# Blockwise causal attention and a swish layer on one core: Q of batches 2 to 7 loaded with even and odd tokens in two planes

## The chip, the cores and the metric

One Trainium2 chip, one core. The metric is device time in microseconds, the median over runs of the whole kernel. Before the change it is 328.6 us (three runs, 328.39 to 328.95).

## What is computed

Attention over 8 batches of 8 heads, 576 tokens and a head width of 64, causal in blocks of 64 tokens, and behind it a two-layer block on the 4608 rows of 512 numbers that the heads give together:

```
scores = (q @ k.T) / 8                      # a token of block i sees the tokens of blocks 0 to i
attn   = softmax(scores)
x      = (attn @ v), heads side by side     # 4608 x 512
h      = x @ w_in                           # 512 -> 2048
g      = h * sigmoid(beta * h)
out    = g @ w_out                          # 2048 -> 512, float32
```

## The kernel before

The kernel is a list of operations that a planner (`Plan.schedule`, line 85) puts in order when the program is built. Each operation has an engine, a planned duration, dependencies and tiles. For DMAs there is a planned transfer time (`xfer`), and the planner models two rings, one for the hardware queue that SyncE (SP) feeds and one for GpSimd's. It hands every engine a fixed sequence; at run time nothing is chosen again, an engine waits on semaphores in that sequence. A change of a planned duration can therefore move any operation of any engine.

The attention works in units: `u = 4 * b + c` is the pair of heads `2c`, `2c + 1` of batch `b`. Batches 0 and 1 load Q and K in one way (line 724) and turn them with TensorE (line 742); the change leaves them alone. For batches 2 to 7 (`QB = 2`), two units, so four heads, go together and are called a quad here. There are 12 quads, and each goes through these steps:

- **Load** (line 765, on SP's queue): the 2304 rows of four heads' Q, 64 floats each, go to a tile `S4` of 128 partitions with 18 rows each, row `128 i + p` in partition `p`. So each piece that a DMA moves is one row of 256 B. K is loaded in the same way. Planned transfer `QKX = 2700` ns for each.
- **Cast** (line 776, GpSimd): four copies of 128x640, for each of two pairs of heads one for Q and one for K, from float32 to bf16, into a tile `QKn`.
- **Transpose** (line 783, a DMA on SP's queue, once all four casts are done): 20 blocks of 128x128 from `QKn` into `QKT`, after which the head dimension lies in the partitions, two heads in the two halves. Planned 3250 ns.
- **Scores** (line 837, TensorE; repeated with the weights kept, line 457): three visits for each quad. The two heads of a pair use the upper and the lower half of the array and write to two neighbouring PSUM banks. A visit has 4 or 12 instructions at line 837.
- **Exponential** (line 857, ScalarE): 128x1024 from the two banks to a tile `E`, three for each pair, and a small one of 128x128 (line 872). VectorE then zeroes the corners of the causal mask (lines 865 and 867).
- **Values** (line 1051, TensorE), the reciprocal of the sum (line 1063) and the product with it (line 1070, VectorE) into `xq`.
- **Transpose of the result** into `xT`: for batch 2 by TensorE and VectorE (lines 1099 and 1109), for batches 3 to 7 by a DMA on SP's queue (line 1087).

The second part runs over 9 chunks of 512 rows: `xT` times `w_in` (line 1297), tanh on ScalarE (line 1307), the gate on VectorE (line 1311), and the product with `w_out`: plain for the first chunk (line 1333), by seven products of quarter blocks with sums on VectorE (lines 1178 and 1214) for the others. The priorities (`pr`, line 452, for the attention; `1000 + 100 r + j` for chunk `r`) let the planner interleave the attention of a batch with the second part of chunks about one and a half batches behind.

SP's queue carries in one sequence the loads of Q, K and V, the transposes of Q and K, and those of `xq`. The output goes out on ScalarE's queue, the weights come in on GpSimd's. Two identity matrices are made by GpSimd at the start (lines 472 to 479); `identF` has 128 columns in float32, and its only use is a 16x16 transpose (line 512).

Of the kernel before, what the change touches and what calls it, by code (L numbers as in the profile page):

```python
# [6 lines left out]
f32 = mybir.dt.float32  # L7
# [352 lines left out]
def bass_blockwise_causal_attn__then__act_swish_beta_kernel(  # L360
# [10 lines left out]
    with es:  # L371
# [97 lines left out]
        def mk(fn):  # L469
# [4 lines left out]
            out=identF[:], in_=identF[:], compare_op=ALU.not_equal, fill=1.0, base=0,  # L474
            pattern=[[-1, 128]], channel_multiplier=1)), deps=[c1], prio=-9)
        c3 = P.op("POOL", 260, mk(lambda g: g.memset(identB[:], 0.0)), prio=-10)
# [177 lines left out]
        early6, rows = [], []  # L654
        QKI, QKX = 550, 2700
        for u in range(NU):
# [102 lines left out]
            elif p == 0:  # L759

                for w, (nm, src) in enumerate((("Q", q), ("K", k))):
                    ts = P.tile("S4")

                    def fl(g, e, ts=ts, src=src, b=b, c=c):
                        return [g.dma_start(STh[ts.slot], src[b, 2 * c:2 * c + 4].rearrange("h t d -> (h t) d").rearrange(
                            "(i p) d -> p i d", p=128))]

                    o = P.op("SP", QKI, fl, deps=[o for t in early6 for o in t.users] if b == QB else [],
                             tiles=[ts], xfer=QKX, prio=u, dma=["d_S4", 0, 1])
                    for i in range(2):  # L770
                        ld[nm, u + i] = o
                    for a in range(2):
                        def fn(g, e, ts=ts, tn=tn, a=a, w=w):
                            x = STh[ts.slot][:, 9 * a:9 * a + 5, :]
                            x = bass.AP(x.tensor, x.offset, [x.ap[0], [64, 5], [256, 2], [1, 64]])
                            return g.tensor_copy(  # L776
                                QKn[tn.slot][:].rearrange("p a w n -> p (a w n)")[:, 640 * (2 * a + w):][:, 0:640]
                                .rearrange("p (t h d) -> p t h d", t=5, h=2), x)

                        casts.append(P.op(CAST, 740, fn, deps=[o], tiles=[ts, tn], prio=u))  # L780

                def ft(g, e, tn=tn, td=tt_):
                    return [g.dma_start_transpose(QKT[td.slot][:].rearrange("c a w (t n) -> c (a w t) n", n=128),
                                                  QKn[tn.slot][:].rearrange("p a w n -> p (a w n)")[:, 0:2560])]
# [6 lines left out]
            if b not in JOIN or p == 0:  # L791
# [6 lines left out]
                for grp in visits:  # L798
# [5 lines left out]
                    def fq(g, e, pst=pst, grp=grp, tqk=tqk, b=b):  # L804
# [8 lines left out]
                        while todo[0] or todo[1]:  # L813
# [4 lines left out]
                            m = 128 if t < 4 or b >= QB else 64  # L818
                            if g0 < 3:
# [8 lines left out]
                            x = QKT[tqk.slot][r, uu % 2, 0, q0 + y:q1 + y]  # L828
                            if b and g0 == 1 and (uu, 0) in grp and t == 0:
                                z = again(g, o, keep[h], x)  # L830
                                continue
                            if g0 == 3 and h and last is not None:
# [18 lines left out]
            for g0 in range(4 if b else 3):  # L851
                o, ps = qk[g0]
                if g0 < 3:
                    n = 512 if b or g0 < 2 else 256

                    def fe(g, e, ps=ps, g0=g0, te=te, n=n):
                        return g.activation(E3[es_(te)][:, g0, :, 0:n], PS[:, ps.slot:ps.slot + 2, 0:n], ACT.Exp,  # L857
                                            scale=0.125)
# [10 lines left out]
                else:  # L869
                    def fe(g, e, ps=ps, te=te, p=p):  # L870
                        n = 128 if te.apart else 64
                        return g.activation(E4[es_(te)][:, 0:n], PS[:, ps.slot, n * p:n * p + n], ACT.Exp, scale=0.125)
                    n = 128 if te.apart else 64
# [553 lines left out]
```

## Time and profile before

| | |
|---|---|
| median of three runs | 328.6 us |
| the profiled execution's own time | 329.3 us |
| its span, first to last instruction | 327.5 us |
| TensorE busy in the span | 316.4 us, 97% |
| ScalarE, VectorE, GpSimd busy | 211.8, 219.9, 84.5 us |
| granted TensorE clock | 0.999 of full speed |
| bytes moved | 53.58 MB, 164 GB/s over the span |

The busy time of an engine is the union of its instructions' durations; a matmul's duration overlaps the next one's, so a TensorE that is busy all the time still has small gaps between streams. The profiled execution took 329.3 us, 1.8 us more than its span and 0.7 us more than the median of the runs. DMA-issuing instructions stand under the queue of the engine that issues them (SPq, ACTq, POOLq); their time is the sequencer's, and it is long when the queue is full.

### The profile page before, as it was taken

How to read it: one execution, taken by the hardware profiler on the slowest of the kernel's cores; microseconds unless marked ns; L12 is line 12 of the kernel's file. 1: busy time of each engine (PE TensorE's matmuls, PEld its weight loads, DVE VectorE, ACT ScalarE, POOL GpSimd, SP SyncE). 2: the span in 40 equal slices, each digit the busy share in tenths (PEclk: the TensorE clock that was granted, in tenths of full speed). 3: DMA queues.
4: the chain of work that ended last, by engine and by line, in shares of the span. 5: the costliest groups of instructions: out<-in, count | busy, mean ns of one | idle time of the engine just before them, and what ended most of it. 6: DMA issues, size and time to landing. Idle time of an engine off the chain costs nothing.

```text
span 327.5 us, 7435 instructions
## 1 busy us (share of the span) xinstructions
PE 316.4 (97%) x3101; PEld 200.3 (61%) x3012; DVE 219.9 (67%) x455; ACT 211.8 (65%) x312; POOL 84.5 (26%) x137
## 2 busy tenths in 40 slices
PE   7698999999999999999999999999999999999996
PEld 2454446445786457854776467666666766666695
DVE  5657857578763789368843996659576866666742
ACT  2769891388557886499657866885978454544521
POOL 4768090073073046103520541150000000000000
PEclk9999999999999999999999999999999999999999
DMA  7999999999999999997999999999030310111023
GB/s 224 225 302 233 215 211 199 169 292 189 226 252 221 222 193 218 186 240 152 196 190 241 231 197 195 199 169 152 0 74 2 104 34 32 62 36 35 6 92 128
DMA packets 156706, 53.58 MB, mean 164 GB/s; under 512 B 139120, under 2 KB 156160, under 8 KB 156672
## 3 DMA queue, kind: packets, MB, share of 16 engines
q1 hardware_dynamic: 144112, 40.46, 65.8%
q10 hardware_dynamic: 8336, 8.46, 8.2%
q0 software_dynamic: 4224, 4.19, 7.8%
q8 instruction: 24, 0.39, 0.5%
q14 instruction: 10, 0.08, 0.1%
HBM read 36.71 MB, written 9.44 MB: 141 GB/s over the span
## 4 chain that ended last, share of the span: by engine, by line
PE 83%; DMA 5%; DVE 4%; ACT 4%; issue 2%; SPq 1%; POOL 1%; POOLq 0%
PE PS L1297 34%; PE PS L1214 29%; PE PS L1051 8%; PE PS L837 6%; PE PS L1333 4%; DMA w_in<-in_moe_w_in_dram 3%; ACT E L857 2%; DMA ST<-in_q_dram 2%; DVE gT L1311 1%; ACT th L1307 1%; DVE QKT L752 1%; SPq L724 1%; DMA xT<-xq 1%; PE PS L1099 1%; PE PS L912 0%
## 5 line engine op out<-in xcount | busy, mean ns | idle before, releaser
L1297 PE MATMUL PS<-xT,w_in 128*128 128x512 bf16 x576 | 137.7, 379 | 3.1 <-DMA w_in<-in_moe_w_in_dram 1.2
L1307 ACT ACTIVATE th<-PS,beta 128x512 f32<-128x512 f32 x144 | 97.0, 701 | 54.9 <-PE PS L1297 53.9
L1311 DVE SCALAR_TENSOR_TENSOR gT<-th,PS 128x512 f16<-128x512 f32 x144 | 95.2, 681 | 35.8 <-ACT th L1307 35.4
L857 ACT ACTIVATE E<-PS 128x1024 bf16<-128x1024 f32 (+1 forms) x90 | 87.5, 1014 | 22.4 <-PE PS L837 21.5
L1297 PEld LDWEIGHTS PS<-xT,w_in 128*128 128x128 bf16 x576 | 53.1, 98 | 58.5 <-issue 2.2
L1214 PE MATMUL PS<-w_out,gT 128*128 128x256 f16 x512 | 63.0, 273 | 0.1
L1214 PEld LDWEIGHTS PS<-w_out,gT 128*128 128x128 f16 x512 | 49.0, 98 | 12.1 <-issue 0.8
L776 POOL CAST QKn<-ST 128x640 bf16<-128x640 f32 x48 | 37.0, 771 | 24.9 <-DMA ST<-in_k_dram 13.9
L624 POOL CAST Vn<-Vs 128x640 bf16<-128x640 f32 x24 | 19.6, 815 | 91.7 <-DMA Vs<-in_v_dram 90.6
L1236 ACT ACTIVATE ost<-PS 128x512 f32<-128x512 f32 x32 | 19.3, 604 | 28.5 <-PE PS L1214 28.5
L1214 PE MATMUL PS<-OV 128*128 128x256 f16 (+1 forms) x264 | 31.8, 270 | 0.0
L1051 PEld LDWEIGHTS PS<-Vn,E 128*128 128x128 bf16 x810 | 27.5, 97 | 3.9 <-issue 0.4
L837 PE MATMUL PS<-QKT 64*128 64x448 bf16 (+7 forms) x292 | 28.6, 295 | 0.5 <-ACT E L857 0.5
L1051 PE MATMUL PS<-Vn,E 128*128 128x65 bf16 x810 | 28.4, 193 | 0.0
L1214 PEld LDWEIGHTS PS<-OV 128*128 128x128 f16 x264 | 24.5, 98 | 6.1 <-issue 0.6
L1178 DVE TENSOR_TENSOR OV<-gT 128x1024 f16<-128x1024 f16 x32 | 23.9, 753 | 0.6
L837 PEld LDWEIGHTS PS<-QKT 64*128 64x128 bf16 (+1 forms) x292 | 13.3, 94 | 17.7 <-issue 3.6
L1070 DVE TENSOR_TENSOR xq<-PS,inv 128x640 bf16<-128x640 f32 x28 | 23.0, 820 | 0.5
L1239 DVE SCALAR_TENSOR_TENSOR ost<-PS,ost 128x512 f32<-128x512 f32 x22 | 15.2, 689 | 9.5 <-PE PS L1214 6.9
L865 DVE MEMSET E<- 64x64 uint32 x57 | 6.3, 112 | 17.9 <-ACT E L857 16.0
L1214 PE MATMUL PS<-OV,gT 128*128 128x256 f16 (+1 forms) x136 | 16.0, 266 | 0.0
L1333 PE MATMUL PS<-w_out,gT 128*128 128x512 f16 x64 | 15.3, 379 | 0.0
(106 smaller groups left out, 189.9 us busy)
## 6 DMA issues: line engine op xcount, KB each, us to landing
out_dram<-ost ACTq DMA_DIRECT2D x32, 256.0 KB, 3.9
ST<-in_q_dram SPq DMA_DIRECT2D x12, 576.0 KB, 6.2
ST<-in_k_dram SPq DMA_DIRECT2D x12, 576.0 KB, 7.2
Vs<-in_v_dram SPq DMA_DIRECT2D x24, 256.0 KB, 4.6
ST<-in_q_dram SPq DMA_DIRECT2D x8, 256.0 KB, 5.9
ST<-in_k_dram SPq DMA_DIRECT2D x8, 256.0 KB, 6.1
w_in<-in_moe_w_in_dram POOLq DMA_DIRECT2D x4, 512.0 KB, 8.4
w_out<-in_moe_w_out_dram POOLq DMA_DIRECT2D x4, 512.0 KB, 8.9
```

What stands on the lines that cost most here:

```text
L624: return g.tensor_copy(Vn[t.slot][:, 0:n, g0:g1, 0:64], Vs[ts.slot][:, 0:n, g0:g1, :])
L776: return g.tensor_copy(QKn[tn.slot][:].rearrange("p a w n -> p (a w n)")[:, 640 * (2 * a + w):][:, 0:640] .rearrange("p (t h d) -> p t h d ...
L837: z = g.matmul(o, QKT[tqk.slot][r, uu % 2, 1, k0:k0 + m], x)
L857: return g.activation(E3[es_(te)][:, g0, :, 0:n], PS[:, ps.slot:ps.slot + 2, 0:n], ACT.Exp, scale=0.125)
L1051: z = g.matmul(o, eblk(te, t, i, h), Vn[Tv.slot][:, t, 2 * c + h, 0:65], start=(t == 0), stop=(t == i))
L1070: return g.tensor_tensor(xq[xq_(tx)][:].rearrange("p i (h d) -> p h i d", h=2), both(pv, 0, 64), x, ALU.mult)
L1178: return P.op("DVE", dve_t(SZ * HC / 2), mk(lambda g: g.tensor_tensor(fo(), fx(), fy(), op)), deps=deps, tiles=tiles, prio=prio)
L1214: x = g.matmul(PS[:, pw.slot, HM * w + c0:HM * w + c1], fa()[:, j, 128 * w:128 * w + 128], fb()[:, j, c0:c1], start=first and (pair or w = ...
L1297: z = g.matmul(PS[:, ph.slot, :], w_in[:, c, 128 * j:128 * j + 128], xT[:, c, row % RX:row % RX + RC], start=(c == 0), stop=(c == 3))
L1307: return g.activation(th[tt.slot][:], PS[:, ph.slot, :], ACT.Tanh, scale=beta[:, j:j + 1])
L1311: return g.scalar_tensor_tensor(out=gT[tg.slot][:, j, :], in0=th[tt.slot][:], scalar=1.0, in1=PS[:, ph.slot, :], op0=ALU.add, op1=ALU.mult)
L1333: z = g.matmul(PS[:, po.slot, 0:d1 - d0], gT[tg.slot][:, j, 128 * w:128 * w + 128], w_out[:, j, d0:d1], start=(j == 0), stop=(j == NJ - 1))
```

## The change

For batches 2 to 7, Q is loaded with two neighbouring tokens in each partition, so that a piece is 512 B. The even and the odd tokens of a head then lie in two planes after the cast: a head's 576 tokens start at partition 0, 32, 64 or 96 of their first block of 256 tokens, so three blocks of two planes are kept for each pair of heads, 768 columns where there were 640. The casts of Q become four of 128x384 for each quad instead of two of 128x640. `QKn` and `QKT` grow from 2560 to 2816 columns, so the transpose has 22 blocks. The score matmul reads its moving operand from the two planes and writes the even tokens' scores to the first half of a bank and the odd ones' to the second; the exponential reads the two halves alternating and writes the tokens in their order. K stays as it is. The planned transfer of Q becomes 2000, the planned transpose 3550, a planned Q cast 470. In SBUF, `identF` shrinks to 16 columns and batch 0's tile `QKt` moves into `OV`.

```diff
-        QKn = [sb(f"QKn{i}", [128, 2, 2, 640], bf16) for i in range(NQ)]
-        QKt = [sb("QKt", [128, 2, 256], bf16), OV[:, 512:768].bitcast(bf16).rearrange("p (w n) -> p w n", w=2)]
+        QKnf = [sb(f"QKn{i}", [128, 2816], bf16) for i in range(NQ)]
+        QKn = [x[:, 0:2560].rearrange("p (a w n) -> p a w n", a=2, w=2) for x in QKnf]
+        QKt = [OV[:, z:z + 256].bitcast(bf16).rearrange("p (w n) -> p w n", w=2) for z in (2048, 512)]
-        QKT = [sb(f"QKT{i}", [128, 2, 2, 640], bf16) for i in range(3)]
+        QKTf = [sb(f"QKT{i}", [128, 2816], bf16) for i in range(3)]
+        QKT = [x[:, 0:2560].rearrange("p (a w n) -> p a w n", a=2, w=2) for x in QKTf]
...
-        identF = sb("identF", [128, 128], f32)
+        identF = sb("identF", [128, 16], f32)
...
-        QKI, QKX = 550, 2700
+        QKI, QKX, QKX2 = 550, 2700, 2000
...
+                    def fl(g, e, ts=ts, src=src, b=b, c=c, w=w):
+                        x = src[b, 2 * c:2 * c + 4].rearrange("h t d -> (h t) d")
+                        if w == 0:
+                            return [g.dma_start(STh[ts.slot].rearrange("p (i j) d -> p i (j d)", j=2),
+                                                x.rearrange("(i p j) d -> p i (j d)", p=128, j=2))]
+                        return [g.dma_start(STh[ts.slot], x.rearrange("(i p) d -> p i d", p=128))]
...
-                             tiles=[ts], xfer=QKX, prio=u, dma=["d_S4", 0, 1])
+                             tiles=[ts], xfer=QKX if w else QKX2, prio=u, dma=["d_S4", 0, 1])
...
+                        for j in range(2 - w):
+                            def fn(g, e, ts=ts, tn=tn, a=a, w=w, j=j):
+                                x = STh[ts.slot][:, 9 * a if w else 8 * a + j, :]
+                                x = bass.AP(x.tensor, x.offset, [x.ap[0], [64, 5] if w else [128, 3], [256, 2], [1, 64]])
+                                y = QKnf[tn.slot][:, 1408 * a + 768:1408 * a + 1408] if w else \
+                                    QKnf[tn.slot][:, 1408 * a + 384 * j:1408 * a + 384 * j + 384]
+                                return g.tensor_copy(y.rearrange("p (t h d) -> p t h d", h=2, d=64), x)
+
+                            casts.append(P.op(CAST, 740 if w else 470, fn, deps=[o], tiles=[ts, tn], prio=u))
...
-                turned = [P.op("SP", 3250, ft, deps=casts, tiles=[tt_, tn], xfer=3200, prio=-1, dma=["d_T", 0, 1])]
+                turned = [P.op("SP", 3550, ft, deps=casts, tiles=[tt_, tn], xfer=3500, prio=-1, dma=["d_T", 0, 1])]
...
+                            n2 = (q1 - q0) // 2
+                            if b >= QB and g0 < 3:
+                                o = PS[:, ps.slot + h, :].rearrange("p (j n) -> p j n", j=2)[:, :, off // 2:off // 2 + n2]
...
-                                o = PS[:, ps.slot, k:k + 64]
+                                o = PS[:, ps.slot, k:k + 64].rearrange("p (j n) -> p j n", j=2)
...
+                            if b >= QB:
+                                s0 = 64 * (uu % 2) + 32 * h + q0 // 2
+                                x = QKTf[tqk.slot][r, 1408 * (uu % 2):1408 * (uu % 2) + 1408]
+                                x, kt = x[:, 0:768].rearrange("c (j n) -> c j n", j=2)[:, :, s0:s0 + n2], x[:, 768 + k0:768 + k0 + m]
...
-                            z = g.matmul(o, QKT[tqk.slot][r, uu % 2, 1, k0:k0 + m], x)
+                            z = g.matmul(o, kt, x)
...
+                        if b >= QB:
+                            return g.activation(E3[es_(te)][:, g0].rearrange("p h (n j) -> p h n j", j=2),
+                                                PS[:, ps.slot:ps.slot + 2].rearrange("p h (j n) -> p h n j", j=2), ACT.Exp, scale=0.125)
...
+                        if te.apart:
+                            x, y = x.rearrange("p (h n j) -> p h n j", h=2, j=2), y.rearrange("p (h j n) -> p h n j", h=2, j=2)
+                        return g.activation(x, y, ACT.Exp, scale=0.125)
```

## Rows read from the trace of the kernel before

**Rows 1.** The page: busy time of each engine, and the chain's shares by engine.

```profile
PE 316.4 (97%) x3101; PEld 200.3 (61%) x3012; DVE 219.9 (67%) x455; ACT 211.8 (65%) x312; POOL 84.5 (26%) x137
...
PE 83%; DMA 5%; DVE 4%; ACT 4%; issue 2%; SPq 1%; POOL 1%; POOLq 0%
```

**Rows 2.** Busy time in stretches: length, PE, PEld, DVE, ACT, POOL, clock, DMA share, GB/s.

```profile
35.00:222.00 187.00, 184.88 (x1884) 115.33 (x1837) 128.17 (x274) 132.81 (x196) 62.31 (x80) 1.00 1.12 209
45.00:251.00 206.00, 204.25 (x2082) 129.15 (x2033) 143.28 (x300) 145.36 (x214) 58.08 (x75) 1.00 1.01 188
251.00:311.00 60.00, 60.00 (x451) 39.90 (x450) 41.45 (x67) 31.78 (x50) 0.00 (x0) 1.00 0.14 42
```

**Rows 3.** Waits of TensorE's matmuls from 45 us on: total us, times, longest.

```profile
PE PS L1297 <- DVE xT L1109: 0.6, 1, 0.6
PE PS L1297 <- DMA xT<-xq: 0.6, 1, 0.6
PE PS L1297 <- DVE gT L1311: 0.2, 1, 0.2
PE PS L837 <- ACT E L857: 0.2, 1, 0.2
```

**Rows 4.** The two longest of these in TensorE's timeline: start, us, idle before.

```profile
104.32 1.04 PE L1297 MATMUL PS<-xT,w_in 128*128 128x512 bf16 x4 [0.62 <-DVE xT L1109]
...
170.92 1.90 PE L1297 MATMUL PS<-xT,w_in 128*128 128x512 bf16 x8 [0.61 <-DMA xT<-xq]
```

**Rows 5.** DMA view of 2 to 10 us, and of 88.5 to 98 us.

```profile
DMA packets 3353, 2.38 MB, mean 297 GB/s; under 512 B 1310, under 2 KB 3353, under 8 KB 3353
...
DMA packets 7562, 2.35 MB, mean 248 GB/s; under 512 B 7177, under 2 KB 7433, under 8 KB 7561
```

**Rows 6.** SP's queue: start, us the issue took.

```profile
91.20 3.06 SPq L765 DMA_DIRECT2D ST<-in_q_dram  x1
94.30 2.95 SPq L765 DMA_DIRECT2D ST<-in_k_dram  x1
...
128.18 5.42 SPq L783 DMA_TRANSPOSE QKT<-QKn  x1
...
167.23 2.55 SPq L1087 DMA_TRANSPOSE xT<-xq  x2
```

**Rows 7.** The two kinds of transposing DMA: issue ns min/median/max, and landing of the first.

```profile
L783 SPq DMA_TRANSPOSE QKT<-QKn x12: 2989/4772/12334, 49.6 to 219.7; - x12
...
DMA to landing us min/median/max: 5.0/7.6/14.4
...
L1087 SPq DMA_TRANSPOSE xT<-xq x24: 1199/1278/3472, 109.6 to 256.9; - x24
```

**Rows 8.** TensorE's timeline: the first scores from the transpose of 128.18 us.

```profile
141.90 0.39 PE L837 MATMUL PS<-QKT 64*128 64x512 bf16 x2
```

**Rows 9.** GpSimd's casts: ns min/median/max, and the shortest step from Q's to K's.

```profile
L776 POOL CAST QKn<-ST x48: 722/723/1241, 45.1 to 219.0; 128x640 bf16<-128x640 f32 x48
L731 POOL CAST QKn<-ST x14: 610/616/631, 4.3 to 32.2; 128x512 bf16<-128x512 f32 x14
...
99.77 1.51 POOL L776 CAST QKn<-ST 128x640 bf16<-128x640 f32 x2 [1.80 <-DMA ST<-in_q_dram]
101.86 1.51 POOL L776 CAST QKn<-ST 128x640 bf16<-128x640 f32 x2 [0.57 <-DMA ST<-in_k_dram]
```

**Rows 10.** Groups of ScalarE: copies that read four PSUM blocks alternating (L752) and straight (L953).

```profile
L752 ACT ACTIVATE QKT<-PS 128x512 bf16<-128x512 bf16 x1 | 0.6, 597 | 0.1
...
L953 ACT ACTIVATE xT<-PS 128x512 bf16<-128x512 bf16 x1 | 0.6, 597 | 2.1 <-PE PS L946 2.1
```

**Rows 11.** Busy time of 45 to 251 us for line 837, and for line 857.

```profile
45.00:251.00 206.00, 22.62 (x240) 11.24 (x240) 1.00 1.01 188
...
45.00:251.00 206.00, 72.27 (x73) 1.00 1.01 188
```

**Rows 12.** GpSimd at the start: the two steps of identF, and its first cast.

```profile
1.16 0.21 POOL L472 MEMSET identF<- 128x128 f32 x1
...
2.03 0.29 POOL L473 TENSOR_SCALAR_AFFINE_SELECT identF<-identF 128x128 f32<-128x128 f32 x1
...
4.26 0.61 POOL L731 CAST QKn<-ST 128x512 bf16<-128x512 f32 x1 [1.13 <-DMA ST<-in_k_dram]
```

**Rows 13.** Waits of SP's queue: total us, times, longest.

```profile
SPq L1087 <- DVE inv L1063: 31.4, 4, 15.0
SPq L783 <- POOL QKn L776: 27.1, 7, 6.1
```

More of the change, by code (lines that the diff above doesn't have):

```diff
@@ L474, in bass_blockwise_causal_attn__then__act_swish_beta_kernel @@
             out=identF[:], in_=identF[:], compare_op=ALU.not_equal, fill=1.0, base=0,
-            pattern=[[-1, 128]], channel_multiplier=1)), deps=[c1], prio=-9)
+            pattern=[[-1, 16]], channel_multiplier=1)), deps=[c1], prio=-9)
         c3 = P.op("POOL", 260, mk(lambda g: g.memset(identB[:], 0.0)), prio=-10)
@@ L762, in bass_blockwise_causal_attn__then__act_swish_beta_kernel @@
                     ts = P.tile("S4")
-                    def fl(g, e, ts=ts, src=src, b=b, c=c):
-                        return [g.dma_start(STh[ts.slot], src[b, 2 * c:2 * c + 4].rearrange("h t d -> (h t) d").rearrange(
-                            "(i p) d -> p i d", p=128))]
+                    def fl(g, e, ts=ts, src=src, b=b, c=c, w=w):
[4 more added lines that the diff above has]
+                        return [g.dma_start(STh[ts.slot], x.rearrange("(i p) d -> p i d", p=128))]
                     o = P.op("SP", QKI, fl, deps=[o for t in early6 for o in t.users] if b == QB else [],
-                             tiles=[ts], xfer=QKX, prio=u, dma=["d_S4", 0, 1])
+                             tiles=[ts], xfer=QKX if w else QKX2, prio=u, dma=["d_S4", 0, 1])
                     for i in range(2):
@@ L772, in bass_blockwise_causal_attn__then__act_swish_beta_kernel @@
                     for a in range(2):
[L773 to L780, printed above, removed]
+                        for j in range(2 - w):
[6 more added lines that the diff above has]
+                            casts.append(P.op(CAST, 740 if w else 470, fn, deps=[o], tiles=[ts, tn], prio=u))
                 def ft(g, e, tn=tn, td=tt_):
-                    return [g.dma_start_transpose(QKT[td.slot][:].rearrange("c a w (t n) -> c (a w t) n", n=128),
-                                                  QKn[tn.slot][:].rearrange("p a w n -> p (a w n)")[:, 0:2560])]
-                turned = [P.op("SP", 3250, ft, deps=casts, tiles=[tt_, tn], xfer=3200, prio=-1, dma=["d_T", 0, 1])]
+                    return [g.dma_start_transpose(QKTf[td.slot][:].rearrange("c (t n) -> c t n", n=128), QKnf[tn.slot][:])]
+                turned = [P.op("SP", 3550, ft, deps=casts, tiles=[tt_, tn], xfer=3500, prio=-1, dma=["d_T", 0, 1])]
             tqk, cps = tt_, turned
@@ L818, in fq @@
                             m = 128 if t < 4 or b >= QB else 64
-                            if g0 < 3:
+                            n2 = (q1 - q0) // 2
+                            if b >= QB and g0 < 3:
+                                o = PS[:, ps.slot + h, :].rearrange("p (j n) -> p j n", j=2)[:, :, off // 2:off // 2 + n2]
+                            elif g0 < 3:
                                 o = PS[:, ps.slot + h, off:off + q1 - q0]
@@ L827, in fq @@
                             k0 = 128 * t + y * (t < 4)
-                            x = QKT[tqk.slot][r, uu % 2, 0, q0 + y:q1 + y]
+                            if b >= QB:
+                                s0 = 64 * (uu % 2) + 32 * h + q0 // 2
+                                x = QKTf[tqk.slot][r, 1408 * (uu % 2):1408 * (uu % 2) + 1408]
+                                x, kt = x[:, 0:768].rearrange("c (j n) -> c j n", j=2)[:, :, s0:s0 + n2], x[:, 768 + k0:768 + k0 + m]
+                            else:
+                                x, kt = QKT[tqk.slot][r, uu % 2, 0, q0:q1], QKT[tqk.slot][r, uu % 2, 1, k0:k0 + m]
                             if b and g0 == 1 and (uu, 0) in grp and t == 0:
@@ L854, in bass_blockwise_causal_attn__then__act_swish_beta_kernel, with fe @@
                     n = 512 if b or g0 < 2 else 256
-                    def fe(g, e, ps=ps, g0=g0, te=te, n=n):
+                    def fe(g, e, ps=ps, g0=g0, te=te, n=n, b=b):
+                        if b >= QB:
+                            return g.activation(E3[es_(te)][:, g0].rearrange("p h (n j) -> p h n j", j=2),
+                                                PS[:, ps.slot:ps.slot + 2].rearrange("p h (j n) -> p h n j", j=2), ACT.Exp, scale=0.125)
                         return g.activation(E3[es_(te)][:, g0, :, 0:n], PS[:, ps.slot:ps.slot + 2, 0:n], ACT.Exp,
@@ L871, in fe @@
                         n = 128 if te.apart else 64
-                        return g.activation(E4[es_(te)][:, 0:n], PS[:, ps.slot, n * p:n * p + n], ACT.Exp, scale=0.125)
+                        x, y = E4[es_(te)][:, 0:n], PS[:, ps.slot, n * p:n * p + n]
+                        if te.apart:
+                            x, y = x.rearrange("p (h n j) -> p h n j", h=2, j=2), y.rearrange("p (h j n) -> p h n j", h=2, j=2)
+                        return g.activation(x, y, ACT.Exp, scale=0.125)
                     n = 128 if te.apart else 64
```

## The prediction

> **What bounds the kernel now.** I read the page first: TensorE is busy for 316.4 us of the 327.5 us span, and 83% of the chain that ended last is TensorE's, with only 5% for DMAs [rows 1]. A sum over the whole run hides stages, so the table of stretches came next [rows 2]. From 251 us on, when the attention is over, TensorE is busy without a break and the DMAs are nearly idle; nothing of this change reaches that stage except through when it starts. From 45 to 251 us, where the quads are worked on, TensorE is busy for 204.25 of 206.00 us, so 1.75 us are open. ScalarE has 145.36 us of work there and GpSimd 58.08. The DMAs are full at the same time: over 35 to 222 us, the stretch in which the quads are loaded and transposed, their share is 1.12 (packets of several queues overlap) at 209 GB/s. So the resource that the change relieves is full, but the engine that sets the end hardly waits for it. The list of TensorE's waits says how much: 1.6 us from 45 us on, and none for QKT, the tile that the changed load feeds [rows 3]. Two of these waits, 0.62 and 0.61 us, are the second part's first matmul standing on `xT`, the end of a batch's attention [rows 4]. These are the places where a late attention reaches TensorE.
>
> **Q's load.** What a piece costs beside its bytes I take from two stretches in which the DMAs were full: 2.38 MB in 3353 packets at 297 GB/s, 8.0 us, against 2.35 MB in 7562 packets at 248 GB/s, 9.5 us [rows 5]. At nearly the same bytes 4209 more packets took 1.5 us, 0.36 ns each. One load of Q loses 1152 of its 2304 packets: 1152 x 0.36 = 0.41 us. Bounds: nothing, if the bytes set the pace; and half of what a load takes while the queue is full, 2.95 to 3.06 us [rows 6], so 1.5 us, if the pieces alone do. I take 0.41, the only one that varies the pieces at fixed bytes. The Trainium skill (DMA: Bandwidth & Descriptors, Specifications) puts the least piece for the full rate at 512 B and says that below it the engine reads, modifies and writes. By that page the sum would use the upper bound; the two stretches of this trace, with rates 17% apart, speak for the smaller one.
>
> **The transpose.** It grows from 20 to 22 blocks. The shortest issue of 20 is 2.99 us, that of a transpose of 5 blocks 1.20 us [rows 7]: 0.12 us a block by the difference, 0.15 by the whole, and 0.24 by the median of 4.77 us, which has waiting for the queue in it. So two blocks cost 0.24 to 0.48 us, and I take 0.30. A quad's stream on SP's queue is then 0.41 - 0.30 = 0.11 us shorter, with ends of 0.48 us longer and 1.26 us shorter.
>
> **The casts.** From 128x640 at 723 ns and 128x512 at 616 ns [rows 9] a column costs 0.84 ns, so 128x384 costs 509 ns. Q of a quad goes from 2 x 0.72 = 1.44 us to 4 x 0.51 = 2.04 us, 0.6 us more on GpSimd, 7 us over 12 quads. The cover is the wait for K: the transpose needs K's casts too, and these start 2.09 us or more after Q's, as at 99.77 and 101.86 us [rows 9], because K lands later. If that cover goes, a quad's transpose is 0.6 us later. SP's queue already waits for casts at this place, 27.1 us in 7 waits [rows 13], and behind it stand the next loads and the transposes of `xq`.
>
> **What the transpose feeds.** The transpose issued at 128.18 us lands after the median of 7.6 us [rows 6, 7], at 135.8; its first score matmul runs at 141.90 us [rows 8]. That is 6 us of slack, so neither a few tenths earlier nor later reaches TensorE here.
>
> **The exponential.** It reads elements of two PSUM halves in turn. ScalarE has one copy that reads four blocks in turn, 128x512, and one of the same size that reads straight: 597 ns each [rows 10]. So I take nothing. Above, the bound is twice the time for each exponential: 73 of them are 72.27 us [rows 11].
>
> **The score matmul.** Columns and instructions stay as many; the moving operand and the output come in two runs of at least 32 columns. No row shows an output in two runs. Below I put nothing, since the columns streamed are the same; above, a second time line 837's 22.62 us [rows 11]. I take nothing, since within a run all stays contiguous. The Trainium skill speaks against the change here: Advanced Engine Details and Errata, PSUM Cachelines, says that an access pattern that is not contiguous slows matmuls significantly. By that page the time would lie near the upper bound, rival D below; the row for reading out of PSUM does not agree with it, for writing no row here decides.
>
> **Small parts.** `identF` with 16 columns saves at most 0.5 us of GpSimd at 1.16 and 2.03 us, where GpSimd waits for the first K until 4.26 us anyway [rows 12]: nothing. `QKt` in another place: nothing, no instruction changes.
>
> **The sum.** The lead adds up quad by quad: when `xT` of batch 2 is awaited at 104.32 us, two quads lie behind it, 0.22 us; at 170.92 us, for batch 4, six, 0.66 us. The waits there are 0.62 and 0.61 us [rows 4], so 0.22 and 0.61 us go, 0.8 us together. The profiled execution took 329.3 us: 328.5 after the change, and since it stood 0.7 us above the median of the three runs, **327.8 us** on that scale. The planner counts 0.7 us less for Q and 0.3 more for the transpose, so its order, too, can bring the attention forward; a new order of the same instructions can also open a wait of the size of those two, which I can't work out from rows and leave to the range.
>
> **Rivals.** A, the forecast: TensorE's waits on `xT` shrink. For it speaks that they are the only waits that a faster stream can reach; against it, that the wait at 170.92 us ends right behind a transpose of `xq` issued in the pair at 167.23 us [rows 6], whose own latency a lighter queue need not shorten. Its own range is 326.9 (all 1.75 us of open time) to 327.9.
> B, a hidden transfer: nothing waits for QKT, its slack of 6 us swallows both signs, and the waits on `xT` are latency, not queueing. Then 328.6, within 0.6 us.
> C, slower: the load is bound by its bytes and saves nothing, while every transpose is longer by 0.30 us and holds SP's in-order queue, with the transposes of `xq` behind it. The place is again `xT`: at batch 2 up to 2 x 0.30 us later, at batch 4 up to 6 x 0.30 = 1.8 us in all. SP's queue waits for other things as well (31.4 us for `xq`, 27.1 us for casts [rows 13]), and in those pauses lateness is made up; half of it, 0.9 us, gives 329.5 on the median's scale (328.6 + 0.9). It decides as soon as a load saves less than the 0.30 us of the transpose.
> D, the PSUM side: the exponential at twice its time would bring ScalarE to 145 + 72 = 217 us in a stretch of 206, the score matmul at twice its time adds 22.6 us to TensorE; from 11 to 23 us more, 340 to 351 and about 345.
> That the change does not do what it says (pieces of 512 B which are split again) is C's case.
>
> **How the numbers follow.** A run-to-run difference of 0.2%, 0.66 us, is about the least that a measurement of this kernel can tell from no change. Chances: A 0.42, B 0.33, C 0.21, D 0.04. A lies over 0.2% below, B within it, C and D above it: faster 0.42, same 0.33, slower 0.25. The range takes in A's lower end with 0.3 us for the order of the plan, 326.6, and C with as much above it, 329.8; D stays out.
>
> **What would show it.** Right: Q's load with 512 B packets and about 13,800 packets fewer in the DMA table; issues of Q shorter than K's beside them; the exponential at 0.99 us (72.27 us / 73 [rows 11]) as before; line 837's group of the same length; the waits of line 1297 on `xT` near 104 and 171 us gone or below 0.3 us; a transpose's shortest issue near 3.3 us. Wrong: exponentials or score matmuls that are longer (D); waits on `xT` that grow, or SP waiting longer for casts (C); new waits of TensorE at other places than `xT`, which would make the written-out order the cause and not the stream; a first stage, before 45 us, of another length, for which I have no term.

## The result: 333.0 us, slower by 1.3%

The changed kernel took 332.96 us (median of 6 runs, 332.39 to 334.25), and the kernel before 328.85 us in the runs beside it: a ratio of 1.013, 95% interval 1.0107 to 1.0154. I forecast 327.8 us, and at the upper end 329.8. The profiled execution took 332.39 us with a span of 330.6 us, 3.1 us longer than before. A ratio here and below compares the fast executions of a kernel with those of the kernel before in the same session, while a median is over all executions, so a ratio need not be the quotient of two medians.

In the lines of the changed kernel L769 is Q's load and L771 K's, L784 the casts, L789 the transpose into `QKT`, L850 the scores, L871 the exponential of batches 2 to 7, L1070 the values, L1106 the transpose into `xT`, L1128 VectorE's copy of batch 2 into `xT`, L1316 `xT` times `w_in`, L1326 the tanh, L1330 the gate, L1233 the product with `w_out`.

**The local costs first**, for they are what I had priced. Busy time of L850 from 45 to 251 us (length, matmuls, weight loads, clock, DMA share, GB/s, as in rows 11):

```profile
45.00:251.00 206.00, 22.02 (x236) 11.04 (x236) 1.00 0.97 190
```

Groups by form: count, busy us, mean ns, idle before:

```profile
L871 ACT ACTIVATE E<-PS 128x1024 bf16<-128x1024 f32 x72 | 71.3, 1027 | 17.2 <-PE PS L850 16.5 <-ACT ost L1255 0.8
...
L784 POOL CAST QKn<-ST 128x384 bf16<-128x384 f32 x48 | 26.3, 548 | 8.2 <-DMA ST<-in_q_dram 5.2 <-POOL Vn L626 0.2
```

The transpose of Q and K, with its landing (columns as in rows 7):

```profile
L789 SPq DMA_TRANSPOSE QKT<-QKn x12: 3340/4346/10387, 50.7 to 215.0; - x12
...
DMA to landing us min/median/max: 5.2/7.2/13.8
```

The score matmul costs 22.02 us / 236 = 93 ns of busy time each, against 22.62 / 240 = 94 ns [rows 11]. The exponential takes 1027 ns; the same form took 1028 ns before. The shortest issue of a transpose grew by 0.35 us, from 2.99 us [rows 7] to 3.34. Nothing here is dearer than I had put it by more than 0.05 us a step.

**Then the end of the chain.** The page of the changed kernel: busy time, DMA packets, its first queue, the chain's shares by engine:

```profile
PE 316.6 (96%) x3101; PEld 199.9 (60%) x3012; DVE 220.6 (67%) x455; ACT 211.9 (64%) x312; POOL 90.7 (27%) x161
...
DMA packets 145954, 54.37 MB, mean 164 GB/s; under 512 B 114544, under 2 KB 145408, under 8 KB 145920
...
q1 hardware_dynamic: 133360, 41.24, 63.7%
...
PE 70%; DVE 10%; ACT 7%; DMA 7%; issue 2%; SPq 1%; POOL 1%; ACTq 0%; POOLq 0%
```

TensorE has the work it had, 316.6 us against 316.4 [rows 1], in a longer span. Its share of the chain fell from 83% [rows 1] to 70%: the chain now goes through VectorE, ScalarE and DMAs at more places. How much is lost this share does not say; the stretches (columns as in rows 2) and the waits do:

```profile
45.00:251.00 206.00, 201.34 (x2057) 127.05 (x2010) 141.88 (x297) 142.32 (x210) 65.08 (x99) 1.00 0.97 190
...
251.00:311.00 60.00, 60.00 (x452) 39.45 (x448) 41.25 (x68) 33.32 (x51) 0.00 (x0) 1.00 0.15 44
```

After 251 us it is as full as before; from 45 to 251 us 4.7 us are open instead of 1.75 [rows 2]. TensorE's waits from 45 us on, as in rows 3, are these:

```profile
PE PS L1316 <- DMA xT<-xq: 2.1, 2, 1.2
PE PS L850 <- ACT E L871: 1.2, 2, 1.0
PE PS L1316 <- DVE xT L1128: 0.6, 1, 0.6
PE PS L1316 <- DVE gT L1330: 0.6, 2, 0.3
```

The large ones in its timeline (columns as in rows 4):

```profile
104.30 1.04 PE L1316 MATMUL PS<-xT,w_in 128*128 128x512 bf16 x4 [0.62 <-DVE xT L1128]
...
141.16 0.39 PE L850 MATMUL PS<-QKT 64*128 64x512 bf16 x2 [1.02 <-ACT E L871]
...
167.22 1.90 PE L1316 MATMUL PS<-xT,w_in 128*128 128x512 bf16 x8 [0.87 <-DMA xT<-xq]
...
202.75 1.90 PE L1316 MATMUL PS<-xT,w_in 128*128 128x512 bf16 x8 [1.22 <-DMA xT<-xq]
```

They come to 2.1 + 1.2 + 0.6 + 0.6 = 4.5 us against 1.6 [rows 3], 2.9 us more, which is nearly all of the 3.1 us of span. None stands on a dearer instruction. What is different is the sequence. TensorE's sequence of operations, 402 without the filler matmuls of the start, is the old one until about 138 us and differs at 114 places from there on. Here is the first such place, in TensorE's timeline of the kernel before:

```profile
138.22 1.92 PE L1214 MATMUL PS<-OV,gT 128*128 128x256 f16 x16
139.98 1.99 PE L1297 MATMUL PS<-xT,w_in 128*128 128x512 bf16 x8
```

and then the scores at 141.90 us [rows 8]. In the timeline of the changed kernel:

```profile
138.22 1.92 PE L1233 MATMUL PS<-OV,gT 128*128 128x256 f16 x16
```

and behind it at once the scores of 141.16 us, with their wait of 1.02 us on `E`. ScalarE's timeline there:

```profile
139.16 1.94 ACT L871 ACTIVATE E<-PS 128x1024 bf16<-128x1024 f32 x2 [0.78 <-ACT ost L1255]
```

The eight products of `xT` and `w_in` that stood between are gone from this place. The scores need the PSUM banks (TensorE's output memory) that the two exponentials of 139.16 us read, and these end at 139.16 + 1.94 = 141.10. Before, the eight matmuls filled that time; now nothing does. The second pattern is the `xT` at 167.22 us. SP's queue of the changed kernel there (columns as in rows 6):

```profile
158.72 3.83 SPq L789 DMA_TRANSPOSE QKT<-QKn  x1
162.59 2.54 SPq L1106 DMA_TRANSPOSE xT<-xq  x2
```

The transposes of `xq` are issued 4.6 us earlier than before (162.59 against 167.23 [rows 6]) and `xT` comes 3.7 us earlier (167.22 against 170.92 [rows 4]). But TensorE's sequence brings it to this visit at 167.22 - 0.87 = 166.35 us, 4.0 us earlier than before (170.92 - 0.61 = 170.31). The plan moved the user forward by more than the queue could move the data.

### The profile page after: what moved, and what is told of

The parts are those of the page before. It is cut to its first block, busy times and chain, and to the rows that moved or that the text cites. A ratio compares the mean times of both kernels' runs of the same rounds, so it can differ in the third digit from the quotient of the medians.

```text
span 330.6 us, 7452 instructions
## 1 busy us (share of the span) xinstructions
PE 316.6 (96%) x3101; PEld 199.9 (60%) x3012; DVE 220.6 (67%) x455; ACT 211.9 (64%) x312; POOL 90.7 (27%) x161
## 2 busy tenths in 40 slices
DMA packets 145954, 54.37 MB, mean 164 GB/s; under 512 B 114544, under 2 KB 145408, under 8 KB 145920
## 4 chain that ended last, share of the span: by engine, by line
PE 70%; DVE 10%; ACT 7%; DMA 7%; issue 2%; SPq 1%; POOL 1%; ACTq 0%; POOLq 0%
PE PS L1316 30%; PE PS L1233 24%; PE PS L1070 6%; PE PS L850 4%; PE PS L1352 4%; DVE gT L1330 4%; DMA w_in<-in_moe_w_in_dram 3%; ACT E L871 3%; DMA xT<-xq 2%; ACT th L1326 2%; ACT E L873 2%; DMA ST<-in_q_dram 2%; DVE gT L1197 2%; DVE xq L1089 1%; DVE OV L1197 1%
## 5 line engine op out<-in xcount | busy, mean ns | idle before, releaser
L1316 PE MATMUL PS<-xT,w_in 128*128 128x512 bf16 x576 | 137.0, 379 | 4.3 <-DMA xT<-xq 2.1
L1326 ACT ACTIVATE th<-PS,beta 128x512 f32<-128x512 f32 x144 | 96.8, 701 | 56.5 <-PE PS L1316 55.6
L1330 DVE SCALAR_TENSOR_TENSOR gT<-th,PS 128x512 f16<-128x512 f32 x144 | 95.0, 682 | 32.6 <-ACT th L1326 32.0
L1316 PEld LDWEIGHTS PS<-xT,w_in 128*128 128x128 bf16 x576 | 52.9, 98 | 61.1 <-DVE gT L1330 3.6
L871 ACT ACTIVATE E<-PS 128x1024 bf16<-128x1024 f32 x72 | 71.3, 1027 | 17.2 <-PE PS L850 16.5
L1233 PE MATMUL PS<-w_out,gT 128*128 128x256 f16 x512 | 62.9, 273 | 0.1
L1233 PEld LDWEIGHTS PS<-w_out,gT 128*128 128x128 f16 x512 | 48.8, 98 | 12.3 <-issue 1.1
L784 POOL CAST QKn<-ST 128x384 bf16<-128x384 f32 (+1 forms) x72 | 44.8, 622 | 12.8 <-DMA ST<-in_q_dram 5.2
L626 POOL CAST Vn<-Vs 128x640 bf16<-128x640 f32 x24 | 18.3, 764 | 92.1 <-DMA Vs<-in_v_dram 91.0
L1233 PE MATMUL PS<-OV 128*128 128x256 f16 (+1 forms) x264 | 31.8, 270 | 0.0
L850 PE MATMUL PS<-QKT 64*128 64x448 bf16 (+8 forms) x292 | 28.7, 295 | 1.6 <-ACT E L871 1.2
L1070 PEld LDWEIGHTS PS<-Vn,E 128*128 128x128 bf16 x810 | 27.3, 97 | 3.4 <-issue 0.4
L1070 PE MATMUL PS<-Vn,E 128*128 128x65 bf16 x810 | 28.2, 193 | 0.0
L1233 PEld LDWEIGHTS PS<-OV 128*128 128x128 f16 x264 | 24.6, 98 | 5.6 <-issue 0.4
L850 PEld LDWEIGHTS PS<-QKT 64*128 64x128 bf16 (+1 forms) x292 | 13.3, 94 | 18.9 <-issue 4.7
L1197 DVE TENSOR_TENSOR OV<-gT 128x1024 f16<-128x1024 f16 x32 | 23.0, 729 | 0.9 <-PE PS L1233 0.6
L873 ACT ACTIVATE E<-PS 128x1024 bf16<-128x1024 f32 (+1 forms) x18 | 16.2, 963 | 8.4 <-PE PS L850 8.4
L1233 PE MATMUL PS<-OV,gT 128*128 128x256 f16 (+1 forms) x136 | 16.1, 266 | 0.0
```

Source lines behind the costliest of these rows:

```text
L784: return g.tensor_copy(y.rearrange("p (t h d) -> p t h d", h=2, d=64), x)
L850: z = g.matmul(o, kt, x)
L871: return g.activation(E3[es_(te)][:, g0].rearrange("p h (n j) -> p h n j", j=2), PS[:, ps.slot:ps.slot + 2].rearrange("p h (j n) -> p h n ...
L1070: z = g.matmul(o, eblk(te, t, i, h), Vn[Tv.slot][:, t, 2 * c + h, 0:65], start=(t == 0), stop=(t == i))
L1197: return P.op("DVE", dve_t(SZ * HC / 2), mk(lambda g: g.tensor_tensor(fo(), fx(), fy(), op)), deps=deps, tiles=tiles, prio=prio)
L1233: x = g.matmul(PS[:, pw.slot, HM * w + c0:HM * w + c1], fa()[:, j, 128 * w:128 * w + 128], fb()[:, j, c0:c1], start=first and (pair or w = ...
```

## The experiments

Two explanations stood against each other: the changed data path (new casts, 22 blocks, scores and exponentials in two planes), or the written-out order which follows from the changed planned durations (2000 for Q, 3550 for the transpose). The planned durations are only numbers for the planner, so path and order can be had apart. Diffs are against the changed kernel where nothing else is said.

### The changed data path in the old order

```diff
-        QKI, QKX, QKX2 = 550, 2700, 2000
+        QKI, QKX, QKX2 = 550, 2700, 2700
...
-                turned = [P.op("SP", 3550, ft, deps=casts, tiles=[tt_, tn], xfer=3500, prio=-1, dma=["d_T", 0, 1])]
+                turned = [P.op("SP", 3250, ft, deps=casts, tiles=[tt_, tn], xfer=3200, prio=-1, dma=["d_T", 0, 1])]
```

> All of the changed data path (512 B pieces of Q, four casts of 384 columns, 22 blocks, two planes, alternating exponential), but the planner is given the planned transfers of before (Q 2700, transpose 3250 and 3200 ns), so that every engine runs its operations in exactly the order of the kernel before. Theory O (the order that the new planned durations bring makes TensorE wait at new places, the data path itself costs nothing): 328.0 to 329.2 us, TensorE's waits from 45 us on 1.0 to 1.8 us. Rival L (the data path is late: longer transposes and more casts): 331 to 333 us, with waits of the second part's first matmul on xT of over 1 us near 167 or 203 us.

Measured: 329.19 us, ratio 1.0009 (0.9985 to 1.0034). Apart from GpSimd's casts, every engine has the sequence of the kernel before. TensorE's waits from 45 us on:

```profile
PE PS L1316 <- ACT E L871: 0.8, 1, 0.8
PE PS L1316 <- issue: 0.8, 5, 0.2
PE PS L850 <- ACT E L871: 0.5, 1, 0.5
PE PS L1316 <- DVE gT L1330: 0.4, 2, 0.2
PE PS L1233 <- DVE OV L1197: 0.2, 1, 0.2
```

Its timeline at the two visits of rows 4:

```profile
104.48 0.81 PE L1316 MATMUL PS<-xT,w_in 128*128 128x512 bf16 x3 [0.84 <-ACT E L871]
...
170.25 1.67 PE L1316 MATMUL PS<-xT,w_in 128*128 128x512 bf16 x7 [0.16 <-issue]
```

Two of these rows have three and seven matmuls where the sequence has four and eight: the first one's record is missing, and the gap ahead of the group is about 0.2 us too long (0.84 - 0.62 = 0.22) and is put down to the wrong releaser. So the 0.84 us is the old 0.62 us on VectorE's `xT`, still there; the 0.61 us at 170.92 us is gone. The 0.8 us put down to `issue` is likely of the same kind: in the stretch from 45 us on it stands only in traces that hold 3064 or 3065 of TensorE's 3101 matmuls. Without it and the 0.22 us the list comes to 1.7 us, as expected. The rival "data path" falls: in the old order all of it together costs nothing that can be measured. Nor does it gain: the profiled execution, 328.58 us, is 0.7 us below that of before, but the medians don't show it.

### The old data path in the new order

Against the kernel before:

```diff
-                             tiles=[ts], xfer=QKX, prio=u, dma=["d_S4", 0, 1])
+                             tiles=[ts], xfer=QKX if w else 2000, prio=u, dma=["d_S4", 0, 1])
...
-                        casts.append(P.op(CAST, 740, fn, deps=[o], tiles=[ts, tn], prio=u))
+                        casts.append(P.op(CAST, 740 if w else 940, fn, deps=[o], tiles=[ts, tn], prio=u))
...
-                turned = [P.op("SP", 3250, ft, deps=casts, tiles=[tt_, tn], xfer=3200, prio=-1, dma=["d_T", 0, 1])]
+                turned = [P.op("SP", 3550, ft, deps=casts, tiles=[tt_, tn], xfer=3500, prio=-1, dma=["d_T", 0, 1])]
```

> The data path of before, but the planner is given the planned durations of the change (Q 2000, transpose 3550 and 3500 ns, casts of Q of the same sum), so that every engine runs the operations in exactly the order of the changed kernel. Theory O: 331.5 to 334 us, with TensorE's waits of about 1 us near 141, 167 and 203 us as in the changed kernel. Rival L: 328.2 to 329.5 us.

Measured: 336.76 us, ratio 1.0229 (1.0189 to 1.027), above what was expected. Every engine apart from GpSimd's casts has the change's sequence. The two longest of its waits:

```profile
PE PS L1297 <- DMA xT<-xq: 4.9, 2, 3.8
PE PS L837 <- ACT E L857: 0.9, 2, 0.7
```

The places in its timeline:

```profile
140.65 0.39 PE L837 MATMUL PS<-QKT 64*128 64x512 bf16 x2 [0.70 <-ACT E L857]
143.40 1.67 PE L1297 MATMUL PS<-xT,w_in 128*128 128x512 bf16 x7 [1.13 <-DMA xT<-xq]
...
170.83 2.25 PE L1297 MATMUL PS<-xT,w_in 128*128 128x512 bf16 x7 [3.78 <-DMA xT<-xq]
```

The order by itself costs 2.3%, and both patterns come with it: the scores that stand on the exponential near 141 us, and `xT`. The two rows on `xT` lack their first matmul, so the 4.9 us are about 4.5. They stand near 143 us and at the visit that the change has at 167.22 us; the one expected near 203 us is not there.

The long wait costs more than its length. Behind it the granted clock was 0.50 from 172 to 175 us, the lower of TensorE's two levels (1.2 of 2.4 GHz); up to 171 us it had been 1.00. The matmuls of the values, and the start of what follows them:

```profile
172.88 1.86 PE L1051 MATMUL PS<-Vn,E 128*128 128x65 bf16 x30
...
175.73 1.04 PE L1214 MATMUL PS<-w_out,gT 128*128 128x256 f16 x8
```

In the change, where the clock stayed at 1.00 behind the wait of 0.87 us, the same two rows are:

```profile
168.96 1.07 PE L1070 MATMUL PS<-Vn,E 128*128 128x65 bf16 x30
...
170.72 1.04 PE L1233 MATMUL PS<-w_out,gT 128*128 128x256 f16 x8
```

From the visit's second matmul to the last of these rows it is 175.73 - 170.83 = 4.9 us here. In the change it is 170.72 - 167.22 = 3.5 us from the first matmul, so about 3.3 from the second. The lower clock cost about 1.6 us.

In this order the data path of the change is worth 336.8 - 333.0 = 3.8 us: by the traces, shorter waits on `xT` and a clock that did not fall. So the change's data path does help; it helps in an order that its own planned durations have made.

### Each planned duration alone

The change with one of the two edits of the first experiment at a time. Transpose planned at 3250 again, Q still at 2000:

> The changed data path, with only Q's planned transfer at 2000 ns and the planned transpose as before. Theory O, if the planned Q is what brings the bad order: 331 to 334 us, with TensorE's waits from 45 us on of over 3 us; if the longer planned transpose is: 328 to 330 us. Rival L: 331 to 333 us as in every order.

Q planned at 2700 again, the transpose still at 3550:

> The changed data path, with only the planned transpose at 3550 and 3500 ns and Q's planned transfer at 2700 as before. Theory O, if the planned Q is what brings the bad order: 328 to 330 us; if the longer planned transpose is: 331 to 334 us. Rival L: 331 to 333 us as in every order.

Measured: Q at 2000 alone 339.43 us, ratio 1.0324 (1.0278 to 1.037), more than expected; the transpose at 3550 alone 331.1 us, ratio 1.0087 (1.006 to 1.0113). The second was expected at 328 to 330 us if the planned Q alone brings the bad order, so that did not hold: either duration by itself makes an order that costs time. With Q at 2000 alone, the longest of TensorE's waits:

```profile
PE PS L1316 <- DMA xT<-xq: 8.1, 3, 4.1
```

In the timeline (each of the three rows lacks its first matmul, so each wait is some 0.2 us too long):

```profile
143.42 0.81 PE L1316 MATMUL PS<-xT,w_in 128*128 128x512 bf16 x3 [2.01 <-DMA xT<-xq]
168.02 0.81 PE L1316 MATMUL PS<-xT,w_in 128*128 128x512 bf16 x3 [2.02 <-DMA xT<-xq]
...
205.55 3.19 PE L1316 MATMUL PS<-xT,w_in 128*128 128x512 bf16 x7 [4.06 <-DMA xT<-xq]
```

In the last of them the granted clock fell, and it was 0.50 from 204 to 210 us: the seven matmuls took 3.19 us; at 143.40 us of the run before, seven took 1.67. The shorter Q makes the larger loss, and the longer transpose takes 6.5 of its 10.7 us back (339.43 to 332.96; 328.77 before). That fits a plan that promises `xT` too early: without the 0.3 us that the transpose adds to each quad the promise is bolder still. The transpose alone has no wait on `xT` from a DMA, but this one, the first pattern:

```profile
141.41 0.39 PE L850 MATMUL PS<-QKT 64*128 64x512 bf16 x2 [1.06 <-ACT E L871]
```

Its profiled execution, 328.78 us, was the lowest of its ten; what the others lose beside that microsecond stays open. A too early promise of `xT` is hardly its cause, for this plan is later than the old one.

### Is it any new order, or a too early promise?

Rival: any other order of 402 operations costs something, by chance. Two plans between, the first with Q at 2400, the second with Q at 2500 and the transpose at 3400 and 3350:

> The changed data path with Q's planned transfer at 2400 ns instead of 2000, the planned transpose as in the change. TensorE's order differs from that of the kernel before at 6 places of 402 instead of 114. Theory O1 (the planned 2000 ns promises Q, and with it xT, earlier than the queue gives them, and the order built on it waits for xT): 328.0 to 329.5 us and no wait on xT of over 0.7 us. Rival O2 (any new order costs some us by chance, whatever the planned Q): 330 to 334 us.

> The changed data path with planned values between: Q 2500, transpose 3400 and 3350 ns. TensorE's order differs from that of the kernel before at 63 places of 402. O1: no wait on xT of over 0.7 us, 327.5 to 329.5 us. O2: 330 to 334 us, with waits on xT or on exponentials of over 1 us.

Measured: 329.55 us, ratio 1.0025 (0.9996 to 1.0054), and 329.94 us, ratio 1.0038 (1.0008 to 1.0067); the first has a single wait on `xT` from a DMA, 0.8 us at 228.93 us (0.6 without the matmul that its row lacks), the second none. Both times lie a little above what was expected, 0.05 and 0.4 us. TensorE's sequence differs from the old one at 6 and 63 places, so the first is hardly a new order. Then, with Q at 2000 and the transpose at 3550 as in the change, only what the plan expects of the transpose into `xT`, from 1100 to 1400 ns, 1300 and 1700:

```diff
-                xt.append(P.op("SP", 1300 * n, fy, deps=nrm + (xt[u - 4:u - 3] if b > XB else []), tiles=[tx], xfer=1100,
+                xt.append(P.op("SP", 1300 * n, fy, deps=nrm + (xt[u - 4:u - 3] if b > XB else []), tiles=[tx], xfer=1400,
```

> The changed kernel, Q planned at 2000, and only the planned transfer of the transposes of xq raised from 1100 to 1400 ns, so that the planner expects xT later. O1: the waits on xT near 167 and 203 us shrink from 2.1 us to under 1 us, and the time lies between 329 and 331.5 us. O2: another order with other waits, 331 to 335 us.

> The changed kernel with the planned transfer of an xT transpose at 1300 ns. TensorE's order differs from the change's at 95 of 402 operations and from that of the 1400 run at 113. Theory O1: a plan that is 0.2 us later for xT lies between 333.0 (1100) and 328.3 (1400): 328.3 to 331.5 us, with 0 to 1.5 us of waits on xT. Rival O2 (chance): anywhere from 329 to 335, with no relation to xT.

> The changed kernel, with the planned transfer of an xT transpose at 1700 ns (1100 in the change, 1400 in the run before this one, which came to 328.3 us). TensorE's order differs from the change's at 137 of 402 operations and from that of the 1400 run at 138, so it is a third order. Theory O1 (the loss is a plan that expects xT earlier than the DMA queue brings it): planning it later still keeps TensorE off xT; under 0.7 us of waits on xT from 45 us on, and 328.0 to 330.5 us (the upper part because a plan that is too late can open waits for other things). Rival O2 (1400 was a lucky order, and every new order costs by chance): 331 to 335, with waits on xT of 2 us or more.

| planned transfer of `xT` | us | ratio, 95% interval |
|---|---|---|
| 1100 (the change) | 332.96 | 1.0107 to 1.0154 |
| 1300 | 330.79 | 1.0023 to 1.0086 |
| 1400 | 328.3 | 0.9978 to 1.0019 |
| 1700 | 329.61 | 0.9983 to 1.0039 |

TensorE's waits from 45 us on, with 1400:

```profile
PE PS L1316 <- ACT E L871: 0.8, 1, 0.8
PE PS L1316 <- issue: 0.8, 5, 0.2
PE PS L1316 <- DVE gT L1330: 0.2, 1, 0.2
PE PS L850 <- ACT E L871: 0.2, 1, 0.2
```

and with 1700:

```profile
PE PS L1316 <- DVE xT L1128: 0.6, 1, 0.6
PE PS L1316 <- DMA xT<-xq: 0.2, 1, 0.2
PE PS L850 <- ACT E L871: 0.2, 1, 0.2
```

One number that no instruction sees, 0.3 us in a plan, brings back the whole 1.3%, and 0.7 us more than was expected of it. The orders with 1400 and 1700 are far from the change's (79 and 137 places) and from each other's (138), and both are as good as before; what they share is that TensorE no longer stands on `xT` from a DMA (0.2 us at most; the 0.8 us of the first list is again the old 0.62 us, in a row that lacks a matmul).

How much this says against chance depends on how new the orders are. The one with 1400 is TensorE's old order in the first 254 of the 402 operations, to about 200 us, and differs from the one with Q at 2500 at 7 places only. The one with 1700 leaves the old order after 187 operations, close to where the change does (184), and costs nothing that can be measured, so an early new order need not cost. But it is the only such one: the four others that leave the old order before 200 us (the change, either planned duration alone, 1300) all cost 0.5 to 3.2%, and the transpose alone does so without a wait on `xT` from a DMA. So chance keeps a part, and its size stays open. The only traced execution with 1300 took 334.82 us, the longest of its ten, with 3.2 us of waits on `xT` from a DMA where at most 1.5 were expected; what those near the median wait for is not known.

### What the data path is worth, order held fixed

K in pieces of 512 B as well, in exactly the change's order (K's tokens then lie in another order than V's, so the attention it computes is not the reference's; the amount of work is the same):

```diff
-                        return [g.dma_start(STh[ts.slot], x.rearrange("(i p) d -> p i d", p=128))]
+                        return [g.dma_start(STh[ts.slot].rearrange("p (i j) d -> p i (j d)", j=2),
+                                            x.rearrange("(i p j) d -> p i (j d)", p=128, j=2))]
```

> Exactly the order of the changed kernel on every engine, but K too is loaded in pieces of 512 B (its tokens then stand in another order, so the scores belong to permuted keys; the amount of work is the same). With pieces of 256 B for both the same order took 336.8 us with 4.9 us of waits on xT, with 512 B for Q 333.0 us with 2.1 us. If the stream on SP's queue is what makes xT late in this order: a further step down, 329.5 to 331.5 us, with waits on xT of under 1.2 us. If the waits on xT are the transposes' own latency: 332.5 to 333.5 us, waits on xT as in the changed kernel.

Measured: 329.18 us, ratio 1.003 (1.0012 to 1.0048), 0.3 us below what was expected. Two of its waits (its lines stand one higher):

```profile
PE PS L851 <- ACT E L872: 0.8, 2, 0.7
PE PS L1317 <- DMA xT<-xq: 0.6, 1, 0.6
```

The first queue on its page:

```profile
q1 hardware_dynamic: 119536, 41.24, 62.3%
```

The row of the 0.6 us lacks a matmul as well, so it is 0.4. So one order with three data paths: pieces of Q and K of 256 and 256 B, 512 and 256, 512 and 512 give 336.8, 333.0 and 329.2 us, with about 4.5, 2.1 and 0.4 us of waits on `xT` from a DMA. A plan that expects too much costs less when the queue delivers more. Last, the old data path in the order of 1400:

> Q in 256 B pieces, 20 blocks, contiguous scores and exponential, as before the change, but in exactly the order of the run with xT planned at 1400 ns (328.3 us with the changed layout). It tells what the changed data path is worth in an order that suits the queue. Theory O1: the order leaves room, so the slower stream costs little: 328.0 to 330.0 us, and at most 1 us of waits on xT. Rival O3 (the new orders need the faster stream, and the change pays in them): 331 to 336, with 2 to 5 us of waits on xT, as the old layout had in the change's own order (336.8 us, 4.9 us).

Measured: 329.44 us, ratio 1.0015 (0.9982 to 1.0048), beside 328.3 us (0.9978 to 1.0019) of the changed path; the intervals overlap. At most 1 us of waits on `xT` was expected, and only the old one on VectorE is left:

```profile
PE PS L1297 <- DVE xT L1109: 0.6, 1, 0.6
PE PS L1297 <- DVE gT L1311: 0.2, 1, 0.2
PE PS L837 <- ACT E L857: 0.2, 1, 0.2
```

Where the order leaves the queue room, the change's data path is worth at most what can't be measured. No version beat the kernel before: the best, 1400, equals it.

## Why the prediction was wrong

**The step that failed** stands at the end of its sum: "a new order of the same instructions can also open a wait of the size of those two, which I can't work out from rows and leave to the range". It opened three large ones (1.02 us on an exponential, 0.87 and 1.22 us on `xT`), not one, and with the old data path that order alone was worth 8.0 us (336.76 - 328.77). I had treated the order as scatter around a sum of local costs. It was the largest term of the change, and it had a sign: the plan had been told 0.7 us less for each load of Q, against 0.3 us more for the transpose, and so brought `xT` and the scores forward. The sum's method, subtracting old waits at their old places, holds only where the sequence stays; in the old sequence the forecast of 327.8 us came to 329.19, within its range but with none of the 0.8 us of gain.

Step by step:

- **Q's load, 0.41 us each.** Right in sign; the size is not settled. The page's share of the first queue times the span is the time its packets took on 16 engines. In three pairs of the same order, old path then new, it fell from 215.5 to 214.1 us (65.8% of 327.5, 65.5% of 326.8), from 213.8 to 210.6 and from 213.1 to 205.4 (65.3% of 326.3, 62.8% of 327.0): 1.4, 3.2 and 7.7 us, single executions, where 12 x 0.11 = 1.3 was forecast with the transposes in it. K in 512 B, in the change's order and with no block added, took off a further 6.4 us (210.6 to 204.2), or 0.53 us a load. But the same changed path in its other orders had between 199.8 us (60.0% of 333.0, with 1300) and 214.3 (65.5% of 327.2, with Q at 2400), so a single difference of this sum does not fix the price. With the 0.30 us priced for each transpose added back, the three pairs give 0.4, 0.6 and 0.9 us a load. The upper bound of 1.5 us a load, which I had set beside the rule of the Trainium skill (DMA: Bandwidth & Descriptors, Specifications) on pieces under 512 B, was not reached in any of them. The median landing of Q itself moved by no clear sign: 6.2 to 5.8, 6.0 to 6.3 and 6.5 to 6.3 us in the three pairs.
- **The transpose, +0.30 us.** +0.35 by the shortest issue. What I missed is that its packets grow as well: the table has 10,752 fewer packets (156,706 - 145,954), not 13,800, so 3,072 came in, 256 for each transpose.
- **The casts, 509 ns.** 507 ns the shortest, 548 the mean. The cover was not whole. In the change SP's wait for casts at the transpose was 22.9 us instead of 27.1 [rows 13], but that is another order. Within one order, old path then new, it grew each time: from 27.1 to 35.0, 18.4 to 22.9 and 22.9 to 26.1 us. It did not reach TensorE in the old order, where the time is that of before.
- **The exponential and the score matmul, nothing.** Right: 1027 ns against 1028, 93 against 94. D falls, and with it, for this pattern, the rule of the Trainium skill (Advanced Engine Details and Errata, PSUM Cachelines): an output in two runs of 32 columns or more did not slow the matmul, and reading two halves alternating did not slow ScalarE.
- **The lead, 0.22 us at 104.32 and 0.61 us at 170.92.** The first was wrong: 0.62 us in the change as before, for this wait ends with TensorE's own transposes and VectorE's copies of batch 2, and it was 0.6 us in all five traces that lack no matmuls. The second went in the old order with the new path, but the medians don't show it.
- **The rivals.** C has the right side and named `xT`, but its mechanism fell: with the same longer transposes in the old order nothing is lost, although its sign, SP waiting longer for casts, is there in every pair of one order. B, a transfer that is hidden anyway, is what the data path alone does. The sign that I had named for a wrong forecast was the one that came: "new waits of TensorE at other places than `xT`, which would make the written-out order the cause and not the stream". It was half of it; waits on `xT` at other times were the other half, and those too came from the order.

Why 2000 was too little is argued, not shown by itself: it promises 0.7 us less a load, which is inside the 0.4 to 0.9 us of the three pairs. Plans at 2400 and 2500 brought the time to within 0.4% of before, but they also bring the old order back, wholly or for its first 200 us. What is shown is that this order makes TensorE wait, and that the waits on `xT` shrink with a later plan for `xT` or a faster queue.

## What to carry to other kernels

Where a planner writes the order, a changed planned duration is an edit to every engine's program: price it as a part of its own, by compiling the new data path in the old order and the old one in the new, before any local cost is believed. A duration given to a planner is a promise to the engine that sets the end; taking 0.7 us off it for each load cost more here than the load could gain. Planning `xT` 0.3 or 0.6 us later cost nothing that could be measured, but a later plan is not safe by itself: 0.3 us more for the transpose of Q and K, with Q as before, cost 0.9%. When a span grows and the busy time does not, look up the new waits in the timeline and compare what stood at that place before.

## What the runs showed that I had not expected

- The loss by pieces: in one fixed, too early order, the change's data path was worth 3.8 us and K in larger pieces another 3.8 (336.8, 333.0, 329.2), the first in part by the clock; in the old order the change's data path was worth nothing that could be measured. Here the value of a transfer depended more on the order around it than on itself.
- With the waits listed at 3.78 and 4.06 us TensorE's granted clock fell to 0.50, for at least 3 and 6 us; with the 0.87 and 1.22 us of the change it stayed at 1.00.
- Two blocks more in a transposing DMA add 256 packets: 3,072 over 12 transposes, with 0.79 MB more moved (54.37 against 53.58 MB).
- Missing records shift a wait's releaser: 0.62 us on VectorE's `xT` in one trace is 0.84 us on ScalarE's `E` in another of the same order, with one matmul less in the row.
